# A two-layer long convolution with a token router: decay powers by ScalarE's Exp, statistics over whole rows, routers that merge the last half chunk, and a renewed order

## The chip, the core and the metric

One core of a Trainium2 chip. Its engines are PE (TensorE, matrix products), DVE (VectorE), ACT (ScalarE), POOL (GpSimd) and SP (SyncE, which here only issues transfers). Each takes the instructions of its own queue in order; between engines there are semaphores. The metric is the device time of one execution in microseconds (us), as the median of several runs.

## The reference

For x of 2048 tokens by 512 channels, a block A and a block B are applied twice, each with the same parameters:

```python
x = x + A(layernorm(x));  x = x + B(layernorm(x));  x = x + A(layernorm(x));  x = x + B(layernorm(x))

def A(u):     # a long convolution per channel; 128 modes n per channel d
    dt = exp(log_dt)
    A = -exp(log_A_real) + 1j * A_imag
    C = (C_real + 1j * C_imag) * dt
    K[d, l] = 2 * sum_n real(C[d, n] * exp(A[d, n] * dt[d] * l))       # l = 0 .. 2047
    return irfft(rfft(u, 4096) * rfft(K, 4096))[:2048] + u * D_skip    # along the tokens

def B(x):     # a feed-forward block on the two tokens with the highest score
    r = x @ w_r
    idx = argsort(-r)[:2]
    y = (silu(x[idx] @ w_gate) * (x[idx] @ w_up)) @ w_down * sigmoid(r[idx])
    return x + scatter(y at idx)
```

w_gate and w_up are 512 x 1792. The taps K are the same in both layers, so their spectra are computed once.

## The kernel before

**Chunks.** The 512 channels are cut into four chunks of 128. A chunk of x is a tile of 128 partitions (two groups of 64 tokens) x 16 tokens j x 128 channels.

**Setup of the taps** (`setup`, once for chunk 0 on tiles of 128 x 128, called `su`; once for chunks 1 to 3 on tiles of 128 x 384, called `su_w`, `su_bigB`, `su_w3b`; partitions are the modes). `mx`, `g1` are the modulus and the phase of C, from Abs, a reciprocal, Arctan and Sin on ACT and a row of operations on POOL (L597 to L621). `al` is -exp(log_A_real) x dt: the exponential is a polynomial of some dozen DVE operations, `exp_` (L519 to L528), and L613 is the product with -dt. From these come planes, two numbers wide (`t`). The phase's planes are integers (L624 to L637, L648; `ip`, `bi`), shifted by a bit from one to the next. The decay's planes hold exp(al x 2^k) for lags that are powers of two: two Tanh on ACT (L614, L615), DVE's 1 - tanh (L639), reciprocal (L640) and product (L641) give exp(.) - 1, five squarings (L655) the next powers, and ACT's Identity with a bias of one (L652) writes each of the six planes. For chunk 0 the planes stay in SBUF (`eight`, `far`, `f32s`, the latter a factor for the last third); for the others they go to DRAM (`prd`, `pid`) and come back chunk by chunk (`load_near`, `load_far`). `planes` (L505 to L514) multiplies or adds them up to all 8 low and 24 high lags: ACT copies, POOL combines.

**K-steps.** 32 of them, 16 channels each, eight to a chunk. ACT copies the first lags (L679, L691), POOL adds the phases (`ph`, L683) and multiplies the decays (`mg`, L697, L702), ACT takes Sin, Abs and Sin for the cosine (`tr`, L713, L707, L716), DVE multiplies (`sc`, L724, L726, L731), PE contracts over the modes (L739), ACT copies the taps (L743), DVE adds the skip (L746), PE transforms (`kq`, L759), and ACT turns it to `gk` (L769). `ph`, `mg` and `sc` have two buffers each, so a K-step can be two ahead at most. After a chunk's eight K-steps PE multiplies them up to the chunk's spectrum (`kx`, L792).

**Convolution.** The chunk is normalized (`z`, L852), transformed (`zf`, L859), transposed on DVE (L863), transformed again (`pu`, L782), multiplied by the spectrum (`p`, L872; `y`, L885, L887), transformed back (`pv`, L893), and copied and transposed (L904, `vt`), and the last product is added to x (L912).

**First norm.** x is loaded once more by chunks (`x0`, two buffers of two tags); DVE takes statistics of each chunk and j (L1016, 64 instructions on 128 elements), joins a token's four (L1023, 16 aggregates) and `rsqrt` (L960 and following) ends it.

**Routers** (`choose`, one per layer). The last chunk comes in two halves of 64 channels: `half_stats` (L943) writes statistics of a half, so a token has five sets of six numbers in `stt`: chunks 0 to 2 and two halves. Each set holds count, mean and sum of squared deviations of the elements at even and at odd places. L1328 joins the five (30 numbers wide, 16 aggregates). `half_dots` gives the products with w_r, by ACT (with a sum over the elements) or DVE (L950). Then come Copy and Sqrt on ACT (L1333, L1335), the score (L1337 to L1351), the two highest (from L1354), the gather of their tokens by DMA, and the feed-forward products.

**Order.** Each engine's order is written out. A table `PLAN` has for each kind of work (a lane: `trig`, `back_mm`, `stat0`) a number for each of its instructions or groups; `put_in` and `put_all` collect them with their numbers, `run` sorts by number and issues, and `in_order` chains each engine's instructions so that no scheduler moves them. The lanes named with `e_` and `t_` are the last chunk of the first and the second layer, `r1` and `r2` the routers.

## Time and profile before

| what | value |
|---|---|
| runs | 546.96, 547.36, 551.83 us; median 547.36 |
| profiled execution | 550.92 us, of which 549.1 is the span from first to last instruction |
| granted clock of PE, mean | 0.969 |
| matrix products' loads and products | 5428 each |
| DVE instructions | 1036 |
| ACT instructions | 849 |
| moved by DMA | 115.77 MB, 211 GB/s in the mean |

The profile has busy times by engine, the span in 40 slices with a digit for the tenths of busy time, groups of instructions by source line (busy time, mean duration of one, idle time of the engine just before them and who ended it), waits, the chain of waits that ended last, and timelines (start, duration, engine, line, output<-input, count; in brackets the idle time before and what released it). L655 is line 655 of the kernel before. An engine's busy time is the time in which at least one of its instructions ran; two neighbours on a queue can overlap by some tens of ns, so a sum of durations may be above it. The profiled execution is one run, here 3.6 us above the median.

### The profile page before, as it was taken

Reading aid. Unit: us, or ns where it says so; the run is one execution under the profiler, and the core shown is the slowest. Engines: PE = TensorE matmul, PEld = TensorE weight load, DVE = VectorE, ACT = ScalarE, POOL = GpSimd, SP = SyncE. Lnnn points to the kernel's source line nnn. Section 1 sums busy time; section 2 is a strip of 40 time slices with the busy share of each in tenths; the row PEclk is TensorE's granted clock in tenths of the full one; section 3 lists DMA queues with packets and bytes.
Section 4 is the critical chain, followed back from the end, with each engine's and each line's share of the span. In section 5 each row is a group of like instructions: output and inputs, shape, how many; then the busy total and the mean of one; then the engine's idle time right before and its main releaser. Section 6 shows DMA issues by size and latency. Waiting matters only on the chain. (4 is left out here: it accounts for less than half of the span.)

```text
span 549.1 us, 14180 instructions
## 1 busy us (share of the span) xinstructions
PE 434.6 (79%) x5428; PEld 340.4 (62%) x5428; DVE 440.7 (80%) x1036; ACT 383.2 (70%) x849; POOL 343.5 (63%) x364
## 2 busy tenths in 40 slices
PE   1001246797999999999999997499999999998388
PEld 1001235586997898778884973266777878774145
DVE  7999999875798899988989558775765789889841
ACT  5427788996999989788773644614466873779893
POOL 2789796899589866766630692306704778889200
PEclk9999999998999999999999999799999999999659
DMA  7520363797768568696567859970781847676843
GB/s 272 221 100 10 135 212 125 214 330 203 188 163 280 162 170 255 184 304 180 128 188 255 329 194 416 414 259 16 229 289 66 289 120 236 188 263 231 306 172 137
DMA packets 67308, 115.77 MB, mean 211 GB/s; under 512 B 8708, under 2 KB 50984, under 8 KB 62504
## 3 DMA queue, kind: packets, MB, share of 16 engines
q1 hardware_dynamic: 67112, 114.85, 63.3%
q8 instruction: 43, 0.70, 0.5%
q14 instruction: 25, 0.20, 0.1%
q0 software_dynamic: 128, 0.02, 0.0%
HBM read 68.83 MB, written 39.72 MB: 198 GB/s over the span
## 5 line engine op out<-in xcount | busy, mean ns | idle before, releaser
L887 POOL TENSOR_TENSOR y<-p 64x256 f32<-64x256 f32 x76 | 57.7, 760 | 65.2 <-DVE p L872 42.1
L739 PE MATMUL pk<-sc 128*32 128x64 f32 x2048 | 39.4, 235 | 55.3 <-DVE sc L731 39.0
L731 DVE TENSOR_TENSOR sc<-tr,mg 128x1024 f32<-128x1024 f32 x64 | 77.2, 1210 | 2.3 <-POOL mg L702 1.5
L739 PEld LDWEIGHTS pk<-sc 128*32 128x32 f32 x2048 | 33.9, 120 | 67.3 <-ACT tr L713 38.7
L683 POOL TENSOR_TENSOR ph<-eight,far 128x768 int32<-128x768 int32 x32 | 53.1, 1663 | 15.8 <-ACT tr L716 14.7
L697 POOL TENSOR_TENSOR mg<-eight,far 128x768 f32<-128x768 f32 x32 | 55.4, 1731 | 9.4 <-DVE sc L726 6.6
L859 PE MATMUL zf<-z,d 128*128 128x256 f32 x192 | 54.8, 418 | 1.1 <-ACT z L852 0.6
L1104 ACT ACTIVATE w<-pv 128x512 f32<-128x512 f32 x48 | 28.3, 592 | 38.0 <-PE pv L893 19.4
L863 DVE STREAM_TRANSPOSE g<-zf 128x512 f32<-128x512 f32 x64 | 45.4, 712 | 11.6 <-PE zf L859 10.2
L759 PE MATMUL kq<-d1k,kt 128*64 128x128 f32 x512 | 38.6, 298 | 14.3 <-DVE kt L746 13.5
L872 DVE TENSOR_TENSOR p<-pu,kf 128x1024 f32<-128x1024 f32 x32 | 38.8, 1218 | 12.6 <-PE pu L782 6.1
L893 PE MATMUL pv<-y,w 128*128 128x128 f32 x320 | 45.4, 284 | 2.8 <-POOL y L885 1.8
L893 PEld LDWEIGHTS pv<-y,w 128*128 128x128 f32 x320 | 40.0, 191 | 11.6 <-issue 5.3
L702 POOL TENSOR_TENSOR mg<-mg,f32s 128x512 f32<-128x512 f32 x32 | 34.8, 1087 | 17.2 <-ACT mg L691 13.0
L759 PEld LDWEIGHTS kq<-d1k,kt 128*64 128x64 f32 x512 | 30.4, 148 | 23.6 <-DVE kt L746 17.3
L782 PE MATMUL pu<-g,w 128*64 128x128 f32 x640 | 42.7, 278 | 1.1 <-DVE g L863 1.0
L859 PEld LDWEIGHTS zf<-z,d 128*128 128x128 f32 x192 | 35.0, 201 | 12.0 <-DVE g L863 2.7
L782 PEld LDWEIGHTS pu<-g,w 128*64 128x64 f32 x640 | 36.6, 134 | 8.5 <-issue 4.2
L885 POOL TENSOR_TENSOR y<-p 64x256 f32<-64x256 f32 x52 | 38.7, 744 | 3.2
L841 PE MATMUL pv<-p,w 128*128 128x128 f32 x192 | 38.6, 283 | 0.0
L841 PE MATMUL pv<-p,w3b 128*128 128x128 f32 x192 | 38.2, 282 | 0.0
L716 ACT ACTIVATE tr<-ph,cst 128x1024 f32<-128x1024 f32 x32 | 35.7, 1116 | 2.6 <-DVE sc L726 2.1
(392 smaller groups left out, 1176.8 us busy)
## 6 DMA issues: line engine op xcount, KB each, us to landing
vd<-w SPq DMA_DIRECT2D x48, 256.0 KB, 2.4
v<-vd SPq DMA_DIRECT2D x24, 512.0 KB, 5.9
kf<-kfd SPq DMA_DIRECT2D x16, 512.0 KB, 4.6
wd<-in_wd SPq DMA_DIRECT2D x4, 2048.0 KB, 9.6
ks<-kd SPq DMA_DIRECT2D x48, 128.0 KB, 3.2
kfd<-kd SPq DMA_DIRECT2D x24, 256.0 KB, 6.2
x<-in_x SPq DMA_DIRECT2D x4, 1024.0 KB, 4.7
w<-in_w SPq DMA_DIRECT2D x2, 2048.0 KB, 9.6
```

The costliest lines, as they stand in the source:

```text
L683: G.tensor_tensor(self.ph[:, :, 8:32].rearrange("p d (k i) -> p d k i", k=3), self.first(0).rearrange("p d (o i) -> p d o i", o=1).to_broa ...
L697: G.tensor_tensor(mg[:, :, 0:2, 8:32].rearrange("p d t (k i) -> p d t k i", k=3), self.first(1).rearrange("p (d t o) i -> p d t o i", t=2, ...
L731: V.tensor_tensor(sc.rearrange("p d (t i) -> p d t i", t=3)[:, :, 0:3:2, :], t, self.mg[:, :, 0:3:2, :], op=OP.mult)
L739: T.matmul(self.pk[32 * g : 32 * g + 32, e, :], t[:, 0:32], t[:, 32:96], start=k == 1, stop=k == 0, tile_position=(0, 32 * g))
L759: T.matmul(self.pq[64 * ri : 64 * ri + 64, e].rearrange("p k g -> p (k g)"), self.kt[:, e].rearrange("p h b -> p (h b)"), d1k[:, 128 * ri ...
L782: T.matmul(pt[64 * par : 64 * par + 64, ri, q, :], w2[:, k1, 64 * ri : 64 * ri + 64], col(src, k1), start=True, stop=True, tile_position=( ...
L841: T.matmul(pv[:, k, :], w[:, j, :], p[:, t, k % 2, k // 2, :], start=t == 0, stop=t == 1)
L859: T.matmul(pf[:, 16 * s : 16 * s + 16, :], d1[:, 128 * s : 128 * s + 128], z[:, :, 16 * q : 16 * q + 16], start=True, stop=True)
L863: V.transpose(g[:, :, 16 * q : 16 * q + 16, :].rearrange("p k e t -> p e k t"), pf.rearrange("p (k t) e -> p e k t", t=2))
L872: V.tensor_tensor(pp, pu.rearrange("p (o r) q e -> p o r (q e)", o=1).to_broadcast([128, 2, 2, 2 * CH]), kf.rearrange("p r (o q) e -> p r ...
L887: E.tensor_tensor(y[0:64, :, par, :], p[0][ls, 0], p[1][ls, 1], op=OP.subtract)
L893: T.matmul(pv[:, k, :], w3[:, 4 * gi + k, :], y[:, k // 2, k % 2, :], start=True, stop=True)
```

## The change

**Decay planes.** `al` is exp on ACT (L595 of the changed kernel), and each of the six planes is written by two Exps on ACT, one for each of its two numbers, with the scale of its power: 12 to a setup (L641). Tanh, 1 - tanh, reciprocal, product, squarings and the Identity copies go, and `exp_` remains for dt alone. In the setup of chunks 1 to 3 the planes alternate over three buffers, not two.

**First norm.** A new input `xr` holds x with whole rows (128 x 16 x 512, the same values). Each of four loads brings four j with all 512 channels; one statistics instruction takes a row (16 in all, L1005). The mean and variance come from the even and odd halves by five operations on 128 x 16 (L1013 to L1021) instead of 16 aggregates.

**Routers.** 16 aggregates over the first four sets (24 numbers, `most_stats`, L932) leave `choose` for lanes of their own (`e_ma`, `t_ma`); the fifth set, the last half chunk, is merged in by ten operations on 128 x 16 (L1332 to L1350), of which the last gives the variance that Sqrt reads.

**Order.** All numbers of `PLAN` are new.

```diff
 PLAN = dict(
-    first=[24, 123],
+    first=[13, 40],
...
+    t_ma=[1012, 1019, 993, 1015, 989, 1020, 1013, 1001, 1018, 990, 1007, 1028, 992, 1010, 988, 1000],
...
             def fplane(k):
-                return direct_plane(1, k) if direct else half(pair(10 + 2 * (k % 2)))
+                return direct_plane(1, k) if direct else half(pair((10, 12, 6)[k % 3] if k else 0))
...
-            S += exp_(V, al, lr, h.bitcast(I32), at_(6), at_(7))
+            S.append(lambda: A.activation(al, lr, AF.Exp))
...
-            S.append(lambda pa=pa: A.activation(pa[:, :, 1], al, AF.Tanh, scale=0.5))
-            S.append(lambda pa=pa: A.activation(pa[:, :, 0], al, AF.Tanh, scale=32.0))
...
-            S.append(lambda pa=pa, pb=pb: V.tensor_scalar(pb, pa, -1.0, 1.0, op0=OP.mult, op1=OP.add))
-            S.append(lambda pb=pb: V.reciprocal(pb, pb))
-            S.append(lambda pa=pa, pb=pb: V.scalar_tensor_tensor(pb, pa, 2.0, pb, op0=OP.mult, op1=OP.mult))
...
             for k in range(1, 7):
                 d = fplane(k)
-                S.append(lambda d=d, pb=pb: A.activation(d, half(pb), AF.Identity, bias=onet))
+                for t, by in ((1, 1.0), (0, 64.0)):
+                    S.append(lambda d=d, t=t, by=by * 2.0 ** (k - 1): A.activation(d[:, :, :, t], hv(al), AF.Exp, scale=by))
                 put(prd, k, d)
-                if k < 6:
-                    S.append(lambda pa=pa, pb=pb: V.scalar_tensor_tensor(pa, pb, 2.0, pb, op0=OP.add, op1=OP.mult))
-                    pa, pb = pb, pa
...
+        def most_stats(mva, stt, j):
+            V.bn_aggr(mva[:, j, :], stt[:, j, 0:4, :].rearrange("p c k -> p (c k)"))
...
-        def first_load(c):
-            x0[c] = sb.tile([128, 16, CH], F32, name=f"x0_{c}", tag=("xc", "z")[c % 2], bufs=1)
-            dma_chunk(x0[c], x, c, True)
+        def first_load(r):
+            x0[r] = sb.tile([128, 4, D], F32, name=f"x0_{r}", tag=("xc", "z")[r % 2], bufs=1)
+            nc.sync.dma_start(x0[r].rearrange("p j e -> p (j e)"), xr[:, 4 * r * D : 4 * (r + 1) * D])
 
-        def first_stats(c, j):
-            V.bn_stats(st0[:, j, c, :], x0[c][:, j, :])
+        def first_stats(j):
+            V.bn_stats(st0[:, j, 0, :], x0[j // 4][:, j % 4, :])
...
         def first_table():
-            mv0 = st([128, 16, 2], "mv0")
-            for j in range(16):
-                V.bn_aggr(mv0[:, j, :], st0[:, j, 0:4].rearrange("p c k -> p (c k)"))
-                yield
-            yield from rsqrt(rs0, mv0[:, :, 1], [128, 16], "rq0")
+            mv0 = st([128, 2, 16], "mv0")
+            me, qe, mo, qo = (st0[:, :, 0, k] for k in (1, 2, 4, 5))
+            add, df, q, var = mv0[:, 0], mv0[:, 1], rs0, bz0
+            V.tensor_tensor(df, me, mo, op=OP.subtract)
...
+            V.scalar_tensor_tensor(var, q, 1.0 / D, df, op0=OP.mult, op1=OP.add)
+            yield
+            yield from rsqrt(rs0, var, [128, 16], "rq0")
...
-                self.mv = mv = st([128, 16, 2], f"mv{i + 1}")
-                for j in range(16):
-                    V.bn_aggr(mv[:, j, :], self.stt[:, j, :, :].rearrange("p c k -> p (c k)"))
-                    yield
+                self.mv = mv = mvs[i]
                 mean, var = mv[:, :, 0], mv[:, :, 1]
+                me, qe, mo, qo = (self.stt[:, :, 4, k] for k in (1, 2, 4, 5))
+                w, q, df, dl = (small([128, 16]) for _ in range(4))
+                part = CH // 2 / D
+                V.tensor_tensor(w, me, mo, op=OP.add)
...
+                V.tensor_tensor(var, q, dl, op=OP.add)
+                yield
```

Three places of the order. The first is ACT's queue ahead of and at the first Sin of the taps (`tr_0`). `su` numbers are tiles of chunk 0's setup, `su_w`, `su_bigB`, `su_w3b` those of chunks 1 to 3; `f32s` and `far_98` are planes of the decay. Before:

```order
20 L652 ACTIVATE su_111<-su_111,cst 128x256 x3
21 L679 ACTIVATE ph_274<-eight_0_244 128x32x16
22 L505 ACTIVATE eight_0_278<-su_111 128x128
23 L603 ACTIVATE su_bigB<-su_bigB 128x384
24 L679 ACTIVATE ph_302<-eight_0_244 128x32x16
25 L652 ACTIVATE far_98<-su_111,cst 128x2x128 x2
26 L691 ACTIVATE mg_336<-eight_0_278 128x16x2x8
27 L652 ACTIVATE f32s<-su_111,cst 128x256
28 L713 ACTIVATE tr_0_340<-ph_274 128x1024
```

After:

```order
21 L498 ACTIVATE eight_0_238<-su_113 128x128
22 L641 ACTIVATE su_w_108<-su_bigB 128x384
23 L593 ACT_TABLE_LOAD
24 L593 ACTIVATE su_bigB<-su_bigB 128x384
25 L641 ACT_TABLE_LOAD
26 L641 ACTIVATE su_w3b<-su_bigB 128x384
27 L665 ACTIVATE ph_253<-eight_0_233 128x32x16
28 L641 ACTIVATE far_98<-su_113 128x2x64
29 L665 ACTIVATE ph_258<-eight_0_233 128x32x16
30 L641 ACTIVATE far_98<-su_113 128x2x64
31 L699 ACT_TABLE_LOAD
32 L699 ACTIVATE tr_0_270<-ph_253 128x1024
```

The plane `f32s` stood as the last before the Sin and is now the first plane written, eighteen rows ahead of it; two Exps of the later chunks and three table loads stand among these rows.

The second is DVE's queue behind the last operation on chunk 0's phase (L648 before, L636 after). Before:

```order
60 L648 TENSOR_SCALAR su_111<-su_111 128x256
61 L637 TENSOR_SCALAR su_111<-su_111 128x256
62 L601 TENSOR_TENSOR su_bigB<-su_bigB 128x384
63 L1016 BN_STATS stt_102<-x_1_164 128x6 x2
64 L640 RECIPROCAL su_111<-su_111 128x256
65 L641 SCALAR_TENSOR_TENSOR su_111<-su_111 128x256
66 L655 SCALAR_TENSOR_TENSOR su_111<-su_111 128x256
67 L521 SCALAR_TENSOR_TENSOR su_w_108<-su_bigB,su_w_108 128x384
68 L655 SCALAR_TENSOR_TENSOR su_111<-su_111 128x256
69 L522 SCALAR_TENSOR_TENSOR su_w_108<-su_bigB,su_w_108 128x384
70 L643 SCALAR_TENSOR_TENSOR su_111<-su_111,dtb 128x128
71 L655 SCALAR_TENSOR_TENSOR su_111<-su_111 128x256
```

After:

```order
41 L636 TENSOR_SCALAR su_113<-su_113 128x256
42 L631 SCALAR_TENSOR_TENSOR su_113<-su_113,dtb 128x128
43 L606 SCALAR_TENSOR_TENSOR su_bigB<-su_bigB,dtb 128x384
44 L1005 BN_STATS stt_102<-x_1_170 128x6 x2
45 L1005 BN_STATS stt_102<-x_0_247 128x6 x3
46 L594 TENSOR_TENSOR su_bigB<-su_bigB 128x384
47 L1005 BN_STATS stt_102<-x_0_247 128x6
48 L1005 BN_STATS stt_102<-x_3_263 128x6 x3
49 L1005 BN_STATS stt_102<-x_2_272 128x6 x2
50 L710 SCALAR_TENSOR_TENSOR sc_283<-tr_0_270,mg_277 128x16x32
```

Eight rows with eleven row-wide statistics and three operations of the setups lie between the phase and the first product of a K-step (L710); before, the rest of the planes, most of the second polynomial and 35 statistics lay there.

The third is DVE's queue in the second router, behind the last transpose. Before:

```order
767 L943 BN_STATS stt_5023<-xw 128x6
768 L1154 BN_STATS stt_5023<-z_1_4365 128x6
769 L943 BN_STATS stt_5023<-xw 128x6 x3
770 L1328 BN_AGGR mv_5955<-stt_5023 128x2 x7
771 L950 TENSOR_REDUCE rdt_5024<-jw_1_1_6008 128x8
772 L1337 TENSOR_REDUCE b_8_6022<-rdt_5024 128x16
```

After:

```order
704 L890 STREAM_TRANSPOSE vt_3_5_5809<-v_3_5570 128x16x16x2
705 L929 BN_STATS stt_4901<-xw 128x6 x6
706 L1152 BN_STATS stt_4901<-x_0_4589 128x6
707 L929 BN_STATS stt_4901<-xw 128x6 x2
708 L932 BN_AGGR mv_112<-stt_4901 128x2 x5
709 L929 BN_STATS stt_4901<-xw 128x6 x4
710 L932 BN_AGGR mv_112<-stt_4901 128x2 x2
711 L939 TENSOR_REDUCE rdt_4902<-jw_1_1_5864 128x8
712 L929 BN_STATS stt_4901<-xw 128x6
713 L932 BN_AGGR mv_112<-stt_4901 128x2
714 L929 BN_STATS stt_4901<-xw 128x6 x2
715 L932 BN_AGGR mv_112<-stt_4901 128x2
```

The 16 aggregates (L932) stand behind the last transpose in the changed kernel too, among the statistics of the second half; the rest of both follows these rows and then, as rows 725 to 734, the ten merge operations. The reduction of the dots (L939) is now ahead of the last aggregates.

More of the change, by code (lines that the diff above doesn't have):

```diff
@@ L407, in in_order, with build @@
             prev[i.engine] = i
-def build(tc, x, lar, aim, cr, ci, ldt, dsk, wr, wg, wu, wd, d1_h, d1k_h, d4_h, w2_h, w3_h, w3b_h, sm_h, out):
+def build(tc, x, xr, lar, aim, cr, ci, ldt, dsk, wr, wg, wu, wd, d1_h, d1k_h, d4_h, w2_h, w3_h, w3b_h, sm_h, out):
     nc = tc.nc
@@ L557, in setup @@
             crt, cit, im, lr, sw, mx = (at_(i) for i in range(6))
-            pa, pb, pc, ip = pair(6), pair(8), pair(26), pair(28).bitcast(I32)
-            ar, ai, w, at, al, h = (at_(i) for i in range(20, 26))
+            pc, ip = pair(26), pair(28).bitcast(I32)
+            ar, ai, w, at, al = (at_(i) for i in range(20, 25))
             def half(t):
@@ L1174, in build @@
         wp = None
+        mvs = [st([128, 16, 2], f"mv{i + 1}") for i in range(2)]
         cu = [Conv(c, 0, x, (rs0, bz0), (), st1, rd1, "A", "B") for c in range(4)]
@@ L1187, in build @@
             put_in("x0", first_load, c)
-            for j in range(16):
-                put_in("stat0", first_stats, c, j)
+            for j in range(4):
+                put_in("stat0", first_stats, 4 * c + j)
         for k in range(6):
@@ L1325, in choose @@
                 i, rdt, small, psum = self.i, self.rdt, self.small, self.psum
-                self.mv = mv = st([128, 16, 2], f"mv{i + 1}")
-                for j in range(16):
-                    V.bn_aggr(mv[:, j, :], self.stt[:, j, :, :].rearrange("p c k -> p (c k)"))
-                    yield
+                self.mv = mv = mvs[i]
                 mean, var = mv[:, :, 0], mv[:, :, 1]
+                me, qe, mo, qo = (self.stt[:, :, 4, k] for k in (1, 2, 4, 5))
+                w, q, df, dl = (small([128, 16]) for _ in range(4))
+                part = CH // 2 / D
+                V.tensor_tensor(w, me, mo, op=OP.add)
+                yield
+                V.tensor_tensor(df, me, mo, op=OP.subtract)
+                yield
+                V.tensor_tensor(q, qe, qo, op=OP.add)
+                yield
+                V.scalar_tensor_tensor(dl, w, 0.5, mean, op0=OP.mult, op1=OP.subtract)
+                yield
+                V.scalar_tensor_tensor(df, df, part / 4, df, op0=OP.mult, op1=OP.mult)
+                yield
+                V.scalar_tensor_tensor(q, var, D - CH // 2, q, op0=OP.mult, op1=OP.add)
+                yield
+                V.scalar_tensor_tensor(mean, dl, part, mean, op0=OP.mult, op1=OP.add)
+                yield
+                V.scalar_tensor_tensor(dl, dl, part * (1 - part), dl, op0=OP.mult, op1=OP.mult)
+                yield
+                V.scalar_tensor_tensor(q, q, 1.0 / D, df, op0=OP.mult, op1=OP.add)
+                yield
+                V.tensor_tensor(var, q, dl, op=OP.add)
+                yield
                 both = small([128, 2, 16])
@@ L1333, in choose @@
                 A.activation(both[:, 0], mean, AF.Copy, scale=-1.0)
-                w, q = (small([128, 16]) for _ in range(2))
                 A.activation(q, var, AF.Sqrt, bias=epst)
-                dot, nd, r = (small([128, 16]) for _ in range(3))
+                dot, nd, r = small([128, 16]), df, dl
                 V.tensor_reduce(dot, rdt, axis=AX, op=OP.add)
@@ L1801, in layout @@
         "x": u.reshape(NCH * L, CH),
+        "xr": f("A_u").reshape(64, 2, 16, D).transpose(1, 0, 2, 3).reshape(128, 16 * D),
         "lar": f("A_log_A_real").T,
```

312 lines of the change are left out of this document (161 added, 151 removed), and 88 rows, old and new, of tables (decay, norm, out, prod_b).

## The prediction

> **What bounds the kernel now.** I read the page first: the busy shares, and the span in 40 slices of 13.7 us.
>
> ```profile
> span 549.1 us, 14180 instructions
> PE 434.6 (79%) x5428; PEld 340.4 (62%) x5428; DVE 440.7 (80%) x1036; ACT 383.2 (70%) x849; POOL 343.5 (63%) x364
> PE   1001246797999999999999997499999999998388
> DVE  7999999875798899988989558775765789889841
> ```
>
> No engine is busy all the time, and DVE and PE stand level, so the averages decide nothing. The slices do: for the first eight (110 us) PE is nearly idle and DVE is at 9, afterwards PE is at 9 nearly throughout, but for two hollows where the routers are. So I cut the span at the first Sin of the kernel taps, at the first product of spectra on PE, and at 300 us (busy time by window: PE, PEld, DVE, ACT, POOL, then clock, DMA share, GB/s). The fifth row is from a second question over the first two stretches.
>
> ```profile
> 0.00:41.10 41.10, 2.21 (x8) 1.85 (x8) 37.51 (x117) 17.44 (x31) 24.96 (x42) 1.00 0.55 198
> 41.10:112.90 71.80, 34.47 (x668) 27.05 (x669) 67.42 (x124) 60.13 (x94) 60.72 (x52) 1.00 0.46 143
> 112.90:300.00 187.10, 180.34 (x2821) 152.33 (x2820) 161.02 (x324) 156.12 (x267) 126.39 (x109) 0.99 0.73 216
> 300.00:549.10 249.10, 217.62 (x1934) 159.14 (x1932) 174.78 (x474) 149.55 (x461) 131.38 (x163) 0.94 0.64 229
> 0.00:112.90 112.90, 36.69 (x676) 28.90 (x677) 104.93 (x240) 77.57 (x123) 85.68 (x93) 1.00 0.49 163
> ```
>
> Up to 112.9 us DVE works 104.9 us of 112.9: it bounds this stage, and ACT (77.6) and POOL (85.7) have slack. From 112.9 to 300 PE works 180.3 of 187.1 us: it bounds that stage, with 6.8 us idle. The timelines show the two cuts, and what stands before the first Sin:
>
> ```profile
> 38.78 1.85 DVE L655 SCALAR_TENSOR_TENSOR su<-su 128x256 f32<-128x256 f32 x1
> 40.67 0.51 ACT L652 ACTIVATE f32s<-su,cst 128x256 f32<-128x256 f32 x1 [8.68 <-DVE su L655]
> 41.08 1.01 ACT L713 ACTIVATE tr<-ph 128x1024 f32<-128x1024 int32 x1
> 34.96 1.63 POOL L683 TENSOR_TENSOR ph<-eight,far 128x768 int32<-128x768 int32 x1
> 112.90 2.90 PE L792 MATMUL kx<-gk,w 128*128 128x128 f32 x24
> ```
>
> The phase that the Sin reads was there at 36.6, but on ACT's queue the last plane stands before the Sin, and it waited 8.7 us for the last squaring, which DVE's queue holds behind statistics. DVE bounds even the start.
>
> **The change part by part: DVE.** What goes, by groups of instructions (busy us, then mean ns; L943 and 347.75, from the first router, give prices):
>
> ```profile
> L525 DVE SCALAR_TENSOR_TENSOR su_w<-su_w 128x384 f32<-128x384 f32 x5 | 3.9, 786 | 0.1
> L525 DVE SCALAR_TENSOR_TENSOR su<-su 128x128 f32<-128x128 f32 x5 | 1.4, 285 | 0.1
> L521 DVE SCALAR_TENSOR_TENSOR su_w<-su_bigB,su_w 128x384 f32<-128x384 int32 x1 | 0.6, 552 | 0.0
> L640 DVE RECIPROCAL su_w<-su_w 128x768 f32<-128x768 f32 x1 | 4.9, 4942 | 0.0
> L640 DVE RECIPROCAL su<-su 128x256 f32<-128x256 f32 x1 | 1.7, 1735 | 0.0
> L655 DVE SCALAR_TENSOR_TENSOR su_w<-su_w 128x768 f32<-128x768 f32 x5 | 5.3, 1064 | 0.0
> L655 DVE SCALAR_TENSOR_TENSOR su<-su 128x256 f32<-128x256 f32 x5 | 3.5, 706 | 0.0
> L1016 DVE BATCH_NORM_STATS2 stt<-x 128x6 f32<-128x128 f32 x64 | 13.9, 274 | 0.0
> L943 DVE BATCH_NORM_STATS2 stt<-xc 128x6 f32<-128x64 f32 x32 | 4.4, 210 | 0.0
> L1023 DVE BATCH_NORM_AGGREGATE mv<-stt 128x2 f32<-128x24 f32 x16 | 2.7, 221 | 0.1
> 347.75 0.17 DVE L1345 TENSOR_TENSOR b<-b,b 128x16 f32<-128x16 f32 x1
> ```
>
> The two polynomial exponentials: 3.9 + 1.4, and seven more operations each, at some 0.45 wide (the L521 row is at the upper end) and half that narrow, 4.7 together: 10. The planes: 4.9 + 1.7 + 5.3 + 3.5 is 15.4, and four single operations (L639 and L641, on each tile), by the squaring's 1.06 and 0.71 at most 3.5, of which I take 3: 18.4. Neighbours on a queue overlap by a few tens of ns, so of these 28 I count 26.5. First statistics: 64 of 128 elements become 16 of 512. The L943 row has 210 ns for 64 elements, L1016 274 for 128, which makes 1 ns an element; 512 would take 274 + 384, so 16 x 0.66 = 10.5 in place of 13.9. An instruction that starts late in a queue shows a longer time, so the gain lies between 0 and 6; I take 3. The 16 aggregates (2.7) become five operations on 128x16 at 0.2 (0.17 in the row of 347.75): 1.5 less. Together **DVE loses 31 of 104.9 us** up to the cut; 74 remain.
>
> **ACT** gets the exponentials.
>
> ```profile
> L652 ACT ACTIVATE su_w3b<-su_w,cst 128x768 f32<-128x768 f32 x6 | 5.6, 927 | 1.6 <-DVE su_w L641 1.6
> L652 ACT ACTIVATE su<-su,cst 128x256 f32<-128x256 f32 x3 | 1.5, 508 | 1.2 <-DVE su L641 0.9 <-DVE su L655 0.3
> L652 ACT ACTIVATE far<-su,cst 128x256 f32<-128x256 f32 x2 | 0.9, 493 | 0.0
> L614 ACT ACTIVATE su_w<-su_bigB 128x384 f32<-128x384 f32 x1 | 0.6, 554 | 2.0 <-DVE su_bigB L613 2.0
> L614 ACT ACTIVATE su<-su 128x128 f32<-128x128 f32 x1 | 0.3, 320 | 2.0 <-DVE su L613 2.0
> 3.89 0.29 ACT L593 ACTIVATE su<-su 128x128 f32<-128x128 f32 x1
> 4.20 1.28 ACT L600 ACT_TABLE_LOAD   x1
> 7.42 1.28 ACT L603 ACT_TABLE_LOAD   x1
> 8.71 0.31 ACT L603 ACTIVATE su<-su 128x128 f32<-128x128 f32 x1
> ```
>
> Off: 12 plane copies (5.6 + 1.5 + 0.9 + 0.5 for the f32s one) and four Tanh (1.7): 10.2. On: Tanh is the nearest shape and function for an Exp, so 13 of 0.32 and 13 of 0.55 (a plane's two halves, and al): 11.3. Besides, the order has six loads of a function table more and three fewer; at 1.28 each that is 3.9. Together **5 us more**, all before the cut: 82.6.
>
> On this price the Trainium skill, "ScalarE: Activation LUTs", section "What ACT_TABLE_LOAD costs", is dearer: 1283 ns for the load and about 1380 ns for a drain, at every switch. The trace agrees with the first figure only: the load at 4.20 follows an ACTIVATE that ended at 4.18, and the ACTIVATE at 8.71 follows a load that ended at 8.70, so no drain shows. By the page the three loads would come to 8 us (an estimate from its figures), and the forecast would be some 4 us later.
>
> **When PE can start its products.** The first Sin no longer has the 8.7 us wait before it, and on DVE the phase's operations stand ahead of nearly all statistics; with the narrow exponential, four statistics in five and a share of the wide polynomial out of the way, the phase's inputs come some 7 us sooner. Phase at 34.96 - 7 = 28, Sin at 29.6 once it is summed: I take 29, bounds 27 and 34 (two of POOL's eight-plane sums are now ahead of it). By the order's rows up to the Sin, ACT has then done 19 us: 17.4, less 3.5 of copies and Tanh, less 1.5 of wide operations that now come later, plus 3.8 and 1.7 for the Exps ahead of it, plus one load. There remain 82.6 - 19.2 = 63.4. DVE, the bound of this stretch before, idled 71.8 - 67.4 = 4.4 us in it; with as much idle on ACT, PE's first product of spectra comes at 29 + 63.4 + 4.4 = 97. POOL is the next bound (29 + 60.7 = 90), DVE the third (76). So **112.9 becomes 97: 16 us less**. The low bound lets ACT idle 71.8 - 60.1 = 11.7, as it did, and starts the Sin at 34: 109, a gain of 4. The high one has DVE's full relief, 31.
>
> **Past the cut** PE issues the same matrix products in nearly the same sequence, and at 180.3 of 187.1 us it set the pace, so the shift is carried on. The rest of the new order I price at nothing; PE's 6.8 us of idle time in that stage cover it on one side (all gone: 6.8 gained), and on the other a late input costs PE what it lacks. I take 0, bounds -3 and +3, from half that idle time.
>
> **Routers.** What happens where the last half chunk has come:
>
> ```profile
> L1328 DVE BATCH_NORM_AGGREGATE mv<-stt 128x2 f32<-128x30 f32 x32 | 6.0, 251 | 0.0
> 331.68 7.81 DVE L904 STREAM_TRANSPOSE vt<-v 128x512 f32<-128x512 f32 x8 [4.50 <-ACT v L1104]
> 344.73 1.17 DVE L1328 BATCH_NORM_AGGREGATE mv<-stt 128x2 f32<-128x30 f32 x7
> 346.41 0.20 ACT L1333 ACTIVATE b<-mv 128x16 f32<-128x16 f32 x1
> 346.83 0.24 DVE L1337 TENSOR_REDUCE b<-rdt 128x16 f32<-128x80 f32 x1
> ```
>
> Aggregates of 24 numbers need no second half, so they could stand ahead of the last transposes. The order leaves them behind, among the second half's statistics, in both routers. Seven at 30 wide took 1.17 us, 0.167 each; the group of 24 wide above has a mean 30 ns shorter: 16 x 0.03 = 0.5 saved at most. Ten merge operations come on top, 0.17 each as at 347.75 or some 0.1 where they overlap, 1 to 2 us, and Sqrt, which ran beside L1337, now waits for the last of them. Behind it queue the reciprocal, the top-2 search and the gather of tokens, so all is on the path: +1.5 a router, **+3 in all**, bounds 0 (the dots on ACT, which lasted to the row of 346.41, end last anyway) and +5.
>
> **The sum**: span 549.1 - 16 + 0 + 3 = 536.1. The profiled execution took 550.92, 1.8 around its span, and the runs' median of 547.36 is 3.6 below it: 536.1 + 1.8 - 3.6 = 534.3, say **534.5 us**, 2.3% less. A measurement of this kernel can tell about 1%, 5.5 us, from no change.
>
> **Rivals.**
> 1. ACT takes over the bound and eats nearly all. For it: slack of 35 us before, which is now filled, Sin and Exp alternate, and a Sin waits while Exps for other chunks pass. Against it: that work is 63 of the 84 us from 29 to 112.9. Sin at 34, idle 11.7, gain 4; routers +3: 546.5.
> By the Trainium skill, "ScalarE: Activation LUTs", section "Table sets: the hidden batching unit", functions of one set are to be batched, since each change reloads; Exp between Sin and Arctan does the opposite. That speaks for this rival; the rows, without a drain, leave it at 3.9 us.
> 2. DVE's whole relief comes out, since ACT's and POOL's slack suffices: 31 less, 3 more: 519.5. For it: DVE was at 94%. Against: 63 us of ACT work do not fit behind a Sin at 29 before 92.
> 3. Slower. Each engine takes its instructions in a fixed order, so one late input on a new order holds all behind it. Place: chunk 1's K-steps between 100 and 150 us, where PE has to share ACT and POOL with the tap supply:
>
> ```profile
> 120.00:130.00 10.00, 6.38 (x114) 5.57 (x113) 6.22 (x10) 9.18 (x16) 9.69 (x11) 1.00 1.00 307
> ```
>
> There PE works 6.4 of 10 us, with ACT and POOL over 9. Starting PE 16 us sooner leaves them as much less time to run ahead, and such slots may recur. At 3.6 lost in 10 us, 13 gained are gone after 36 us of such supply, and over 52 it is slower by 1%; 70 us of it give 534.5 + 25 = 559.5. Against it: the K-steps' own work is unchanged, and over the whole stage ACT has 31 us idle.
> 4. The merges do what their place would allow, and 16 aggregates vanish behind the dots: 3 less a router than I count, 531.5; it lies inside the forecast's range.
>
> **How the numbers follow.** Forecast with its own range of 527 to 541 (gain 10 to 22, routers 0 to 5, with the 4th rival): 0.64. ACT eats it, 542 to 549: 0.16. DVE's whole relief, below 527: 0.12. Slower by over 1%, above 552.8: 0.08. The range to hold 8 in 10 runs from 522 to 546: it takes in the forecast, two thirds of the first rival and half of the second, and leaves out 0.08 + 0.05 + 0.06. Faster by over 1% (below 541.9): 0.64 + 0.12 = 0.76; within 1%: 0.16; slower: 0.08.
>
> **What would show it.** Right: first Sin near 29 us with no squaring before it; first kx near 97, ACT busier than DVE up to there, DVE near 75 us; the kx-to-300 stage's 187 us unchanged; from the last transpose to L1357 some 1.5 us more in each router. Wrong: DVE still above 90% up to the first kx; a row-wide statistics instruction above 0.9 us; PE idle for over 15 us in the 187 us behind the first kx.

## The result and the profile after

The changed kernel took 534.55 us in the median of four runs (532.35 to 538.73), the kernel before 549.6 beside it. The ratio is 0.9725, 95% interval 0.9679 to 0.9772; in a second comparison, further down, 0.9763 (0.9730 to 0.9796). The forecast of 534.5 us was made against 547.36, a ratio of 0.9765. The ratios leave out executions at a lower clock or more than 1.5% above the fastest of their kernel (in b_rows below, three of ten, two of them at 682 and 765 us). The profiled run has a span of 530.9 us, 18.2 less than the 549.1 of before. That is more than the 13 that the forecast took off the span, and more than the 15.1 between the medians, since it compares one execution with one; the step-by-step account below therefore counts for more than the agreement in the time.

The span in 40 slices (of 13.3 us now) shows the first stage shortened by about a slice:

```profile
PE   1011467999999999999989985899799999998486
DVE  7878779787888899888977479675567689799851
```

The busy time by window, with the cuts at the same events as before (first Sin, first product of spectra, the 249 us before the end; the last row is from a second question):

```profile
0.00:28.50 28.50, 2.05 (x8) 1.78 (x8) 22.50 (x59) 18.03 (x35) 17.70 (x35) 1.00 0.72 249
28.50:97.70 69.20, 32.78 (x669) 25.87 (x670) 56.38 (x84) 63.00 (x103) 65.04 (x59) 1.00 0.54 189
97.70:281.90 184.20, 180.11 (x2833) 151.70 (x2833) 158.40 (x326) 154.83 (x266) 125.91 (x109) 1.00 0.75 207
281.90:530.90 249.00, 217.47 (x1925) 159.51 (x1920) 174.60 (x491) 149.33 (x460) 131.35 (x163) 0.94 0.65 231
0.00:97.70 97.70, 34.82 (x677) 27.65 (x678) 78.88 (x142) 81.03 (x137) 82.74 (x93) 1.00 0.59 206
```

Up to the first product of spectra DVE (third pair of numbers in a row) now works 78.9 us and not 104.9, ACT 81.0 and not 77.6, POOL 82.7 and not 85.7. The three stand level, and in fact POOL works most. The rows for `kx` (duration of one: least, median, greatest; then the start of the first and of the last) give the two ends of the second stage, of before and after:

```profile
L792 PE MATMUL kx<-gk,w x192: 272/275/377, 112.9 to 247.4; 128*128 128x128 f32 x192
```

```profile
L778 PE MATMUL kx<-gk,w x192: 272/275/377, 97.7 to 227.5; 128*128 128x128 f32 x192
```

The first kx comes 15.2 us sooner. From the first to the last it is 134.5 us before, 129.8 after: 4.7 less. The rest, from starts in the two timelines: last kx to first transpose of router 1, 84.3 and 83.8 (0.5 less); from there to the reduction of the dots (L1337, now L1357), 15.1 and 15.8 (0.7 more); to the last transpose of router 2, 158.8 and 159.5 (0.7 more); to its reduction, 9.0 and 10.1 (1.1 more); to the end, 34.5 and 34.2 (0.3 less). The sum is 18.2 us less.

### The profile page after: what moved, and what is told of

The parts are those of the page before. It is cut to its first block, busy times and chain, and to the rows that moved or that the text cites. A ratio compares the mean times of both kernels' runs of the same rounds, so it can differ in the third digit from the quotient of the medians.

```text
span 530.9 us, 14080 instructions
## 1 busy us (share of the span) xinstructions
PE 432.4 (81%) x5428; PEld 338.9 (64%) x5428; DVE 411.9 (78%) x957; ACT 385.2 (73%) x862; POOL 340.0 (64%) x364
## 5 line engine op out<-in xcount | busy, mean ns | idle before, releaser
L683 POOL TENSOR_TENSOR mg<-eight,far 128x768 f32<-128x768 f32 x32 | 53.6, 1674 | 17.7 <-DVE sc L712 10.0
L845 PE MATMUL zf<-z,d 128*128 128x256 f32 x192 | 53.6, 411 | 2.2 <-ACT z L1630 1.1
L1102 ACT ACTIVATE w<-pv 128x512 f32<-128x512 f32 x48 | 28.5, 594 | 35.2 <-PE pv L879 19.1
L879 PE MATMUL pv<-y,w 128*128 128x128 f32 x320 | 47.0, 294 | 4.3 <-POOL y L871 4.3
L879 PEld LDWEIGHTS pv<-y,w 128*128 128x128 f32 x320 | 41.8, 201 | 12.3 <-POOL y L871 9.2
L745 PE MATMUL kq<-d1k,kt 128*64 128x128 f32 x512 | 38.5, 297 | 12.6 <-DVE kt L732 11.2
L745 PEld LDWEIGHTS kq<-d1k,kt 128*64 128x64 f32 x512 | 30.2, 147 | 20.7 <-DVE kt L732 15.6
L699 ACT ACTIVATE tr<-ph 128x1024 f32<-128x1024 int32 x32 | 32.9, 1028 | 4.7 <-DVE sc L717 3.0
## 6 DMA issues: line engine op xcount, KB each, us to landing
ks<-kd SPq DMA_DIRECT2D x48, 128.0 KB, 3.4
```

What stands on the lines that cost most here:

```text
L683: G.tensor_tensor(mg[:, :, 0:2, 8:32].rearrange("p d t (k i) -> p d t k i", k=3), self.first(1).rearrange("p (d t o) i -> p d t o i", t=2, ...
L745: T.matmul(self.pq[64 * ri : 64 * ri + 64, e].rearrange("p k g -> p (k g)"), self.kt[:, e].rearrange("p h b -> p (h b)"), d1k[:, 128 * ri ...
L845: T.matmul(pf[:, 16 * s : 16 * s + 16, :], d1[:, 128 * s : 128 * s + 128], z[:, :, 16 * q : 16 * q + 16], start=True, stop=True)
L879: T.matmul(pv[:, k, :], w3[:, 4 * gi + k, :], y[:, k // 2, k % 2, :], start=True, stop=True)
```

## The experiments

Two kinds of kernels. Those whose name begins with b_ are the kernel before, with its order, and one part of the change; those with a_ are the changed kernel, with something undone or added; after_again is the changed kernel once more. Times to which several expectations refer stand together here, from one profile of each; "kx" is the PE product above.

| kernel | first Sin | first kx | first to last kx | span | ratio to before (interval) |
|---|---|---|---|---|---|
| before | 41.1 | 112.9 | 134.5 | 549.1 | |
| changed | 28.5 | 97.7 | 129.8 | 530.9 | 0.9725 (0.9679 to 0.9772) |
| after_again | 29.2 | 98.5 | 129.6 | 532.0 | 0.9763 (0.9730 to 0.9796) |
| b_exp | 37.9 | 118.4 | 133.9 | 556.6 | 1.0109 (1.0020 to 1.0197) |
| b_rows | 41.8 | 113.7 | 131.7 | 546.3 | 0.9998 (0.9951 to 1.0045) |
| b_both | 37.4 | 117.9 | 130.9 | 548.9 | 1.0155 (1.0048 to 1.0263) |
| b_expb | 37.6 | 115.5 | 133.6 | 551.2 | 1.0040 (0.9997 to 1.0083) |
| a_oldrouter | 28.5 | 99.1 | 130.2 | 532.9 | 0.9832 (0.9745 to 0.9918) |
| a_act | 28.6 | 102.9 | 132.3 | 538.3 | 0.9800 (0.9716 to 0.9885) |
| a_pool | 29.0 | 105.2 | 129.7 | 537.0 | 0.9824 (0.9747 to 0.9901) |
| a_dve | 28.6 | 113.3 | 129.8 | 547.8 | 0.9994 (0.9961 to 1.0026) |
| a_dvebn | 28.7 | 105.1 | 131.0 | 536.3 | 0.9828 (0.9769 to 0.9887) |
| a_best | 27.5 | 99.2 | 131.3 | 537.6 | 0.9789 (0.9750 to 0.9827) |
| a_best2 | 28.2 | 97.7 | 130.4 | 532.3 | 0.9757 (0.9705 to 0.9809) |

Up to the first kx, after_again and a_oldrouter run the same instructions as the changed kernel, yet their first kx comes 0.8 and 1.4 us later. So a difference of 1.4 us or less in that column shows nothing by itself. The three profiles also show where the difference comes from. In the changed kernel DVE waits for the last loaded quarter of x, with the first product of a K-step behind it in its queue. Here is its first instruction after that wait, called DVE's return below, in the changed kernel, after_again, a_oldrouter and a_best:

```profile
32.50 1.29 DVE L1005 BATCH_NORM_STATS2 stt<-x 128x6 f32<-128x512 f32 x2 [3.01 <-DMA x<-in_xr]
33.29 1.29 DVE L1005 BATCH_NORM_STATS2 stt<-x 128x6 f32<-128x512 f32 x2 [3.20 <-DMA x<-in_xr]
33.97 1.28 DVE L1005 BATCH_NORM_STATS2 stt<-x 128x6 f32<-128x512 f32 x2 [2.92 <-DMA x<-in_xr]
34.01 1.29 DVE L1005 BATCH_NORM_STATS2 stt<-x 128x6 f32<-128x512 f32 x2 [2.95 <-DMA x<-in_xr]
```

From DVE's return to the first kx it is 65.1 to 65.2 us in all four, although the first Sin lies anywhere between 27.5 and 29.2. So the first kx of the a_ kernels is better read from DVE's return than from the start of the program:

| kernel | DVE's return | from there to the first kx |
|---|---|---|
| changed | 32.5 | 65.2 |
| after_again | 33.3 | 65.2 |
| a_oldrouter | 34.0 | 65.1 |
| a_best | 34.0 | 65.1 |
| a_best2 | 32.6 | 65.1 |
| a_act | 34.2 | 68.8 |
| a_pool | 34.8 | 70.4 |
| a_dve | 32.6 | 80.7 |
| a_dvebn | 34.2 | 71.0 |

(In a_best2, where two statistics were moved, the instruction after the wait is the first product itself.)

**The Exps without the new order (b_exp).** The lanes' numbers are those of before; steps that fall away do nothing.

```diff
-            S += exp_(V, al, lr, h.bitcast(I32), at_(6), at_(7))
+            S += [lambda: None] * 11
+            S.append(lambda: A.activation(al, lr, AF.Exp))
...
-                S.append(lambda d=d, pb=pb: A.activation(d, half(pb), AF.Identity, bias=onet))
+                def exps(d=d, k=k):
+                    for t, by in ((1, 1.0), (0, 64.0)):
+                        A.activation(d[:, :, :, t], hv(al), AF.Exp, scale=by * 2.0 ** (k - 1))
```

> The kernel before in its own order, with the Exps alone: al and chunk 0's twelve Exps at the place of the Tanhs, the other chunks' at the places of the Identity copies; no polynomial exp on the setups, no reciprocal, no squarings. Theory (DVE bounded the first stage, the relief is what brings the gain): DVE has about 26 us less up to the first kx, but the Exps stand singly among the Sins, 27 table loads in place of 17, so ACT goes from 77.6 to about 91 us up to the first kx; first Sin near 34 instead of 41, first kx at 101 to 107 instead of 112.9, time 6 to 12 us below before. The part after the first kx keeps its length if its gain of 5 us in the changed kernel comes from the order. Rival (the order is what brings the gain): first kx at 110 or later, time within 3 us of before. Second rival (the 5 us behind the first kx come from relieved engines, not from the order): the stretch from the first to the last kx is 130 us instead of 134.5 here too.

It is slower than before, which neither side expected, though the first rival had the first kx at 110 or later. (The profiled execution, at a span of 556.6, is the slowest of its four.) The stretch from the first to the last kx keeps its length (133.9), so the second rival is out. The stretch up to its first kx, in one row, then ACT's first Sin, and ACT's timeline in the middle of the stretch:

```profile
0.00:118.40 118.40, 36.01 (x677) 28.82 (x678) 82.11 (x200) 90.61 (x143) 81.73 (x93) 0.97 0.46 156
```

```profile
37.92 1.03 ACT L717 ACTIVATE tr<-ph 128x1024 f32<-128x1024 int32 x1 [7.32 <-POOL ph L687]
```

```profile
78.91 1.28 ACT L652 ACT_TABLE_LOAD   x1
80.21 0.96 ACT L652 ACTIVATE su_w3b<-su_bigB 128x384 f32<-128x384 f32 x2
81.19 1.28 ACT L720 ACT_TABLE_LOAD   x1
82.48 1.12 ACT L720 ACTIVATE tr<-ph,cst 128x1024 f32<-128x1024 f32 x1
```

DVE has its 23 us less (82.1), ACT its 13 more (90.6), both as foreseen. The first Sin no longer waits for the squarings, but comes only 3.2 us sooner: it now waits 7.3 us, by the trace for POOL, and starts right behind POOL's second phase addition, which ends at 37.89. Then ACT works 70.9 of 80.5 us up to the first kx (60.1 of 71.8 before): for two Exps of 0.96 us together it pays two loads of 1.28. What DVE gains, ACT loses. In the old order the relief of DVE is no gain, and the time says 1.1% of loss.

**The Exps in two groups (b_expb)**: four buffers for the later chunks' planes, and the twelve Exps in two groups of six.

```diff
-                return direct_plane(1, k) if direct else half(pair(10 + 2 * (k % 2)))
+                return direct_plane(1, k) if direct else half(pair((10, 12, 6, 8)[k % 4]))
```

> The kernel before in its own order with the Exps, as in the first such run, but the later chunks' twelve Exps stand in two groups of six (four buffers for the planes), so ACT has 23 table loads and not 27. Theory (ACT bounds that run's first stage, and each load is paid): ACT has 90.6 - 5.1 = 85.5 us up to the first kx, which comes 4 to 5 us sooner, at 113.5 to 114.5 instead of 118.4; time 3 to 6 us below that run. Rival (the loads lie in ACT's waits): first kx within 1 us of 118.4.

The first kx comes at 115.5: 2.9 us sooner for 5.1 us of loads, of which 0.3 us is there at the first Sin already. By this pair of profiles about half of the loads' time was on the path; the rest lay in waits. The first theory's 4 to 5 is too much, the rival's 1 too little. The time is no longer clearly above before.

**The row statistics without the new order (b_rows)**, and **both (b_both)**. In b_rows the two new functions of the first norm stand in the order of before.

> The kernel before in its own order, with the first norm's statistics from whole rows alone (16 statistics for 64, five small operations for 16 aggregates). Theory: DVE bounds the stage and has some 5 us less (13.9 to 10.3 and 2.7 to about 1.0), so the first kx comes 3 to 5 us sooner, time 3 to 5 us less. Rival: statistics fill gaps that DVE has anyway, first kx within 1 us of 112.9, time unchanged.

Nothing: 113.7, ratio 0.9998. But DVE did not get its 5 us either. Its busy time up to the first kx was 103.75 us, 1.2 less, though the 16 statistics took 10.4. The view of DVE and of POOL shows one place where the rest went:

```profile
55.30 1.62 DVE L1027 TENSOR_TENSOR mv<-stt 128x16 f32<-128x16 f32 x1
```

```profile
54.94 1.93 POOL L683 TENSOR_TENSOR ph<-eight,far 128x768 int32<-128x768 int32 x1
```

A subtraction of 128x16 elements, 0.17 us elsewhere, lasts 1.62 and ends at 56.92, just behind POOL's phase addition at 56.87. The next pair of runs on DVE takes this up.

> The kernel before in its own order, with the Exps and the row statistics. Theory: with DVE relieved by 31 us the bound is ACT with its 27 table loads (about 91 us), so the rows add little to the Exps alone: first kx within 2 us of that run, at 100 to 106, time 7 to 13 us below before; the rest to the changed kernel's 97.7 is the order. Rival: both reliefs add up, first kx at 97 or sooner.

It is as b_exp (117.9 against 118.4): the rows add nothing to the first kx. That agrees with the theory of ACT as the bound, but does not show it, for ACT works 90.5 of the 117.9 us; the sizes were wrong, since b_exp itself came out 11 to 17 us later than expected. The step from 117.9 to 97.7 belongs to the new order, with the three plane buffers that it needs.

**The old router (a_oldrouter)**: the 16 aggregates over five sets in `choose`, no merges.

```diff
-            V.bn_aggr(mva[:, j, :], stt[:, j, 0:4, :].rearrange("p c k -> p (c k)"))
+            pass
...
+                for j in range(16):
+                    V.bn_aggr(mv[:, j, :], self.stt[:, j, :, :].rearrange("p c k -> p (c k)"))
```

> The changed kernel with the routers as before: 16 aggregates of all five sets (30 numbers) behind the last statistics and no merges. Theory: the merges cost DVE 1.0 us a router and the narrower aggregates save 0.5 at most, so router 1 is 0.3 to 0.8 us shorter from the last transpose to the reduction of the dots; router 2 waits 1.1 us for ACT's dots and gains nothing: 0 to 1 us below the changed kernel. Rival (the merges pay): 1 us or more longer in each router, 2 to 4 us above the changed kernel.

Router 1 takes 15.8 us from the first transpose to the reduction (15.8 in the changed kernel), router 2 10.0 from the last (10.1). The merges neither cost nor pay more than a tenth of a us. So the 0.7 and 1.1 us that the routers lost against before do not come from the merges; what is left is the place of the work in the order, which no run changed by itself. In router 2 DVE is done with the last merge at 495.6 and waits:

```profile
495.41 0.17 DVE L1350 TENSOR_TENSOR mv<-b,b 128x16 f32<-128x16 f32 x1
496.70 0.24 DVE L1357 TENSOR_REDUCE b<-rdt 128x16 f32<-128x80 f32 x1 [1.12 <-ACT jw L937]
```

**Idle work on one engine (a_act, a_pool, a_dve)**, at one place in each of the first eight K-steps: behind the cosine, behind the decay, behind the last product.

```diff
+        def more(f):
+            f()
+            for _ in range(3):
+                A.activation(scr, scr, AF.Copy)
...
-                put_in("trig", k.trig, n)
+                put_in("trig", (lambda k=k: more(lambda: k.trig(2))) if n == 2 and k.u < 8 else (lambda k=k, n=n: k.trig(n)))
```

> The changed kernel with idle work on ACT: three copies of 128x128 in each of the first eight K-steps, about 0.75 us a K-step, 6 us in all, in a tile of its own. First theory (ACT bounds the changed kernel's first stage, with 81.0 of 97.7 us): the first kx 4.5 to 6 us later, at 102 to 104. Second (POOL does, with 82.7): at most 2 later. Third (no engine alone: two buffers for each tile make a loop over the engines): 2 to 4.5 later.

> The changed kernel with idle work on POOL: two products of 128x128 in each of the first eight K-steps, about 0.9 us a K-step, 7 us in all. First theory (ACT bounds): the first kx at most 2 us later. Second (POOL bounds): 5.5 to 7 later, at 103 to 105. Third (a loop): 2 to 5 later.

> The changed kernel with idle work on DVE: three products of 128x128 in each of the first eight K-steps, about 0.7 us a K-step, 5.6 us in all. First theory (ACT bounds, DVE has been relieved to 78.9 of 97.7 us): the first kx at most 1.5 us later. Second (POOL bounds): the same. Third (a loop): 2 to 4 later. If DVE still bounded, 4.5 to 5.6.

Measured against the changed kernel's 97.7, the first kx comes 5.2, 7.5 and 15.6 us later, but part of that is not the added work: in a_act and a_pool the quarter of x landed 1.7 and 2.3 us later, from a transfer that was issued before the first added instruction ran. Counted from DVE's return it is 3.6 us for 6.3 us more of ACT's busy time (87.3 for 81.0), 5.2 for 6.7 more of POOL's, and 15.5 for 17.9 more of DVE's. Work on each of the three is paid in part, so none of them alone is the bound: the K-steps' pace is set by a chain through all three, and a us on any of them costs 0.6 to 0.9 us. The first theory falls, the second too; the third holds for ACT (2 to 4.5) and nearly for POOL (2 to 5).

The DVE run was far outside of all expectations, and its 24 products say why. Their row in the view by lines has not 5.6 us but 14.1:

```profile
L1230 DVE SCALAR_TENSOR_TENSOR scr<-scr 128x128 f32<-128x128 f32 x24 | 14.1, 589 | 0.5
```

DVE's timeline at the second place, and POOL's at the same time (start, duration):

```profile
37.85 3.59 DVE L1230 SCALAR_TENSOR_TENSOR scr<-scr 128x128 f32<-128x128 f32 x3
41.36 0.68 DVE L1005 BATCH_NORM_STATS2 stt<-x 128x6 f32<-128x512 f32 x1
```

```profile
38.01 1.64 POOL L683 TENSOR_TENSOR mg<-eight,far 128x768 f32<-128x768 f32 x1 [0.74 <-DVE sc L717]
39.61 1.68 POOL L669 TENSOR_TENSOR ph<-eight,far 128x768 int32<-128x768 int32 x1
41.25 1.04 POOL L598 TENSOR_TENSOR su_w<-su_w,su_bigB 128x384 f32<-128x384 f32 x1
```

Three products of nominally 0.9 us together last 3.59 beside two POOL instructions, and end just behind the second's end, at 41.29. Two more triples fall into gaps of POOL (at 45.4 and 90.7) and take 0.93 and 0.92. Not every POOL instruction holds them: at 59.72, beside a TENSOR_SCALAR on POOL (59.30 to 60.47), a product took 0.28.

**The same place, another instruction (a_dvebn)**: `V.bn_stats(scr6, scr)` three times in place of the products.

> The changed kernel with idle work on DVE at the same places as the run with three products in each of the first eight K-steps, but as three statistics instructions of 128x128 into a small tile: one operand from SBUF and not two, nominally as long (0.27 us each). Theory (a product of two SBUF operands on DVE is held up while POOL works, as the products that lasted up to 1.69 us; statistics are not): 24 instructions take 5 to 6.5 us and not 14, and the first kx comes 4 to 6 us later than in the changed kernel, at 102 to 104, not at 113. Rival (the place in the order is what costs): first kx at 110 or later here too.

```profile
L1231 DVE BATCH_NORM_STATS2 scr<-scr 128x6 f32<-128x128 f32 x24 | 6.9, 289 | 0.5
```

24 statistics take 6.9 us at 0.27 to 0.30 each, and the first kx comes at 105.1. Counted from DVE's return that is 5.8 us more than in the changed kernel, within the expected 4 to 6, where the same number of products at the same places cost 15.5. The kind of the instruction decides, not the place; the rival's 110 is not reached. DVE's busy time rose by more than the 6.9, by 11.0 us, since other instructions of its queue got longer too.

The Trainium skill, "GPSIMD Engine Reference", section "8. Key points", says that GpSimd shares its SBUF interfaces with VectorE, with contention for instructions of VectorE in a two-port mode or with two SBUF inputs. The traces agree: the products (two SBUF inputs) were held for up to 1.69 us, the statistics (one input) never above 0.30. That section states no price; here an instruction of 0.29 us took 0.59 in the mean.

**A faster one? (a_best, a_best2).** a_best moves three Exps ahead of the Arctan and the first norm's Sqrt behind a cosine, and gives DVE one more group of dots in the second router.

```diff
-    table=[162, 163, 168, 169, 171, 178, 179, 184, 185, 186, 187, 189, 386],
+    table=[162, 163, 168, 169, 171, 188.1, 188.2, 188.3, 188.4, 188.5, 188.6, 189, 386],
...
-                half_dots(h, k, self.y.pop(("j", h, k)), self.tables()[1], HDOT[h])
+                half_dots(h, k, self.y.pop(("j", h, k)), self.tables()[1], "AV" if self.layer else HDOT[h])
```

> The changed kernel with two table loads fewer up to the first kx (18 in all, not 20): a later chunk's Exp and two of chunk 0's go ahead of the Arctan, and the first norm's Sqrt goes behind a cosine, next to the Exps; and in the second router one more group of eight dots is on DVE, not on ACT. Theory (ACT's time counts in the first stage, as the added copies showed at 0.7 to 0.85 us for one): first Sin at 27.3 instead of 28.5, first kx 1.5 to 2.5 us sooner, at 95.2 to 96.2; in the second router, where DVE waited 1.1 us for ACT's dots, the reduction of the dots comes 0.3 to 0.6 us sooner behind the last transpose; time 2 to 3 us below the changed kernel. Rival (POOL or DVE end last and the loads lie in ACT's waits): first kx within 0.7 us of 97.7.

The first Sin came a us sooner, the first kx did not (99.2), although ACT had 78.5 us of work up to it and not 81.0. The theory's 95 to 96 fails, and the 99.2 is outside of the rival's 0.7 us as well. The quarter of x landed late (34.0), and from DVE's return it was 65.1 us as in the changed kernel: the saved loads lay in ACT's waits, as the rival had it. The second router got 1.6 us longer (11.6 from the last transpose to the reduction). There are two buffers for the products with w_r; POOL's last product now waited for ACT to free one:

```profile
499.09 1.31 POOL L925 TENSOR_TENSOR jw<-xw,wrt 128x512 f32<-128x512 f32 x1 [2.20 <-ACT jw L937]
```

> The changed kernel with the two table loads fewer of the first such run (its router change is left out), and with two statistics of the last loaded quarter of x behind the first K-step's products on DVE, not ahead of them. In the changed kernel DVE waited 3.0 us for that quarter's transfer, with the first product behind it, from 29.5 to 32.5 us; Sin, cosine and decay for that product were there at 32.2. Theory (the K-steps of the first stage are a loop over POOL, ACT and DVE with two buffers, which starts when the first product does, and DVE's late start hid the saved loads): first product at 31 to 32 instead of 33.7, first kx 1 to 2.5 us sooner than in the changed kernel, at 95.2 to 97 (97.7 and 98.5 there), time up to 2 us below it. Rival (the pace is set later in the stage): first kx at 97.5 to 98.5.

The first product came at 32.6, not 33.7, the first kx at 97.7. It is neither faster nor slower than the changed kernel (0.9757 against 0.9725 and 0.9763). DVE's products show where the head start went. In the changed kernel, and behind it in a_best2:

```profile
33.70 0.68 DVE L710 SCALAR_TENSOR_TENSOR sc<-tr,mg 128x512 f32<-128x512 f32 x1
40.67 1.21 DVE L717 TENSOR_TENSOR sc<-tr,mg 128x1024 f32<-128x1024 f32 x1
97.76 1.21 DVE L717 TENSOR_TENSOR sc<-tr,mg 128x1024 f32<-128x1024 f32 x1
```

```profile
32.57 0.69 DVE L710 SCALAR_TENSOR_TENSOR sc<-tr,mg 128x512 f32<-128x512 f32 x1 [2.34 <-POOL mg L683]
40.73 1.21 DVE L717 TENSOR_TENSOR sc<-tr,mg 128x1024 f32<-128x1024 f32 x1
97.77 2.34 DVE L717 TENSOR_TENSOR sc<-tr,mg 128x1024 f32<-128x1024 f32 x2
```

At the second K-step's last product both stand at 40.7, and 57 us later still within 0.01 us, with 2.7 us less work on ACT in one of them. DVE takes up work at the same time in both, in the one when the transfer lands (32.50), in the other when POOL's decay is ready (32.57), and has the same work ahead of it: the statistics that were moved fill the place where the head start was. No version here beats the changed kernel.

**Once more (after_again).**

> The changed kernel once more, unchanged, beside the other two: first kx within 1.5 us of 97.7, the stretch from the first to the last kx within 0.5 us of 129.8, ratio to the kernel before 0.968 to 0.977.

All three came out: 98.5, 129.6, 0.9763.

## Why the prediction was right, and where not

**The first stage: the sizes held, the reason only in part.** First Sin 28.5 (29 foreseen), first kx 97.7 (97), ACT's work up to it 81.0 (82.6). Of the 15.2 us, 12.6 lie ahead of the first Sin, as foreseen (12), and 2.6 behind it (4 foreseen). Of the terms, DVE's relief was 26.0 us, not 31 (27.6 and 24.4 in the two other profiles of the same first stage). The statistics were right: 0.68 us each, 10.3 for 16.

```profile
L1005 DVE BATCH_NORM_STATS2 stt<-x 128x6 f32<-128x512 f32 x16 | 10.3, 679 | 5.0 <-DMA x<-in_xr 5.0
L625 DVE TENSOR_SCALAR su_bigB<-su_w 128x768 int32<-128x768 f32 x1 | 1.3, 1303 | 0.0
```

```profile
L634 DVE TENSOR_SCALAR su_bigB<-su_bigB 128x768 int32<-128x768 f32 x1 | 0.5, 548 | 0.0
```

What was missing is that operations which the change leaves alone got longer: the phase operation of the last two rows (L634 before, L625 after) took 548 ns and now takes 1303, and four others of that setup went the same way, 3.3 us in all, while others got up to 0.7 shorter. The step that summed durations from the rows of before took them as properties of the instructions; these rows and the products in a_dve suggest that they depend on what POOL does meanwhile.

The step "DVE bounds, then ACT does" failed. ACT does not bound the stage: work added to ACT, POOL or DVE costs 0.6 to 0.9 us a us, and two loads less on ACT gained nothing. The three engines are a chain, in which DVE waits for what it has itself set off:

```profile
DVE kt L732 <- ACT kt L729: 7.6, 6, 2.7
DVE stt L1005 <- DMA x<-in_xr: 3.0, 1, 3.0
```

Six times, 7.6 us in all, DVE stood at the skip of a K-step's taps until ACT had copied them. The second row is the quarter of x from above: the forecast had no wait for a transfer in this stage, and the first kx follows the end of that wait, not the first Sin. The sum of 29 + 63.4 + 4.4 used ACT's work as the length of a chain of which ACT's part is the longest but one, and assumed an idle share like DVE's; measured were 28.5, 63.0 and 6.2. POOL, put second with 60.7 us behind the Sin, worked 65.0 there. That the three terms held so well is partly luck.

**The gain was credited to DVE's relief, and without the new order the relief gains nothing.** This is the forecast's largest fault. It read the first Sin and the table loads off the new order's rows, but took DVE as the bound of this stage and its relief as the reason, and priced the rest of the new order, past the first kx, at nothing. With the Exps in the old order the kernel is 1.1% slower; with all of DVE's relief, row statistics included, the first kx is still at 117.9. The wait of 8.7 us for the squarings, on which the forecast built its earlier Sin, is gone there too, but only 3.2 us come out, since a wait of 7.3 us for POOL's phase takes its place. The relief is needed in the new order, though: giving DVE back 18 us (96.8 of busy time, in a_dve) loses the whole of the first stage's gain, 113.3. No run has the new order without the relief, so what the order would do alone is not shown.

The first rival, ACT as the bound, and the rule of the Trainium skill that was weighed there ("ScalarE: Activation LUTs", section "Table sets: the hidden batching unit") fit b_exp: 27 loads, 10 more than before, and the gain gone. The new order has 20 loads, so the rival did not come true for the change. The longer price, with a drain, was not seen in any run: in b_exp too a load ends at 80.19 and the Exp starts at 80.21.

**From the first to the last kx, 4.7 us less where 0 was taken** (bounds -3 and +3); this term was outside of its bounds. Before, PE waited 3.4 us for one product (L833) there; in the changed kernel 0.4 (the same product, now L819). The first row is PE's next instruction behind that wait, the second shows PE's granted clock right after it, 0.52 in the mean (third number from the right):

```profile
129.65 1.15 PE L792 MATMUL pu<-g,w 128*128 128x128 f32 x8 [3.42 <-DVE p L833]
```

```profile
130.85:134.30 3.45, 3.45 (x20) 3.23 (x20) 3.37 (x6) 1.27 (x2) 2.83 (x3) 0.52 0.39 89
```

3.4 us at half the clock are 1.7 us of work lost, and PE's busy time in the whole stretch is 1.9 us longer before (129.5 to 127.7). So the 4.7 are 3.0 of that wait and 1.7 of the clock. b_exp and b_expb show the same pair, a wait of 2.7 and 2.4 us and then some 3.4 us at a clock of 0.50; b_rows and b_both have waits of 2.2 and 1.4, no such stretch, and 128.0 us of busy time. The order is therefore not all of it: with the row statistics alone, in the old order, the stretch fell from 134.5 to 131.7, and from 133.9 in b_exp to 130.9 in b_both. In the eight others with the new order the wait is 0.4 us and the stretch 129.6 to 132.3. That the longer wait brings on the lower clock is suggested by these five profiles, one of each kernel, and not shown.

**Routers: 1.8 us more, not 3**, and for another reason. The ten merges cost nothing that shows (a_oldrouter): in both routers the reduction waits for ACT's dots (0.3 and 1.1 us), which the forecast had named for its lower bound of 0. The sign "1.5 us more from the last transpose" came out in router 2 (1.1 more), not in router 1, where that part got 0.6 shorter and the eight transposes, now with statistics between them, 1.3 longer. The fourth rival is refuted as well; its 531.5 takes 3 us off in all, where its words, 3 less a router, would make it 528.5.

**Slower** (third rival): nothing of it; the taps of chunk 1 were ready, and PE worked 36.7 of the 37.1 us behind the first kx.

**The time.** That 534.55 meets 534.5 so closely is luck. The profiles differ by 18.2 us and not 13, since the term past the cut was missed by 4.7, and the kernel before had a median of 549.6 beside the changed one and not the 547.36 that the forecast started from.

## What to carry to other kernels

Work moved from a full engine to one with slack is worth what the new place in the order makes of it: count the switches that it adds there (here 1.28 us each, two for a pair of Exps of 0.96), and test the move in the old order too before crediting it. When several engines stand within a few us of each other, an engine's total is no bound; add a known amount of idle work to each in turn and read what it costs. Before reading a us or two out of two profiles, look at the same work in a second execution: here the landing of one transfer moved the stage's end by up to 1.4 us, and counting from there made the executions agree within 0.1. And a duration in a profile belongs to its neighbours as well: before an instruction on DVE is priced from a row, look at what POOL did at that time.
